# Output projection of two cached attention blocks: weights taken with a column step of four, and the 128x4 results stored directly

## The chip, the cores and the metric

The kernel runs on one core of a Trainium2 chip. The time is the device time of one execution in microseconds; the median of three runs before the change is 671.81 us (671.5 to 672.41). One execution was also recorded by the hardware profiler; its own time is 671.82 us, and its span, from the first to the last instruction, is 670.0 us.

## The reference

Two attention blocks, A and B, of the same shape decode one token each, and their results are put side by side. Cut to what matters:

```
# for each block: x [1,1,512], k_cache and v_cache [1,32,8192,128], wq [512,4096], wo [4096,512], all bf16
q      = (x @ wq) reshaped to 32 heads of 128
scores = q . k_cache / sqrt(128)            # [32, 8192]
p      = softmax(scores)
o      = p @ v_cache                        # [32, 128]
y      = o reshaped to [1, 4096] @ wo       # [1, 512]
out    = concatenate([y_A, y_B])            # [1, 1, 1024] bf16
```

The two caches of the two blocks are 268 MB, so nearly all that is moved is read once and used once.

## The kernel before, in words

The heads are taken in pairs: 16 pairs of block A (n = 0 to 15), then 16 of block B (n = 16 to 31). For one pair the 128 partitions hold 2 heads times 64 runs of 128 cache rows, so that K and V of a pair are tiles of 128 partitions by 16384 bf16, 4 MB each, in two buffers each (`kn`, `vn`). Every load is issued by SP's DMA queue, in the order written in the program: a K load waits until TensorE has reduced the pair two before it, a V load until the products with V of the pair two before it are done.

The work on a pair: VectorE multiplies K by the broadcast query in four pieces (`plan_mul`, L313). TensorE adds up groups of eight columns through an identity matrix (`plan_red`, L322, two halves of 16 matmuls), VectorE finishes the sums (`plan_sr`, L331) and takes the maximum (L337, L343, L346). TensorE spreads the maximum (L356), ScalarE takes exponentials (`plan_exp`, L367). In the next round TensorE sums the denominators (`plan_sum`, L372) and multiplies the probabilities by V (`plan_pv`, L388, 128 small matmuls with V as weights), and VectorE divides (`plan_o`, L398). Engines run their own instruction lists in the written order and meet through semaphores. TensorE's rounds 1 to 30 are a hardware loop; rounds 31 and 32 stand behind it.

At the start the row x is turned into columns by eight matmuls (L277, weights `xrow[0:1, a, c:D:C]`, which is one partition and a column step of C = 4), and the queries are made from wq (L295).

The output projection is at the end of the program. In round 31 (`L1`), ahead of that round's K work, four relayouts bring finished heads into columns (`plan_relayout`: L423 on VectorE, L427 on TensorE, L429 on VectorE), and `plan_wo(0, 0)` runs block A's whole projection: 128 matmuls (L440) of a 128x128 piece of `wo` as weights by one column of `o2`, four output columns for each of 32 heads, accumulated in `qyp` (128 partitions by 4). When it is done, SP issues block B's `wo` into the same buffer `wbuf` in five loads (16, 8, 4, 2 and 2 heads, `load_wo`), and VectorE rounds `qyp` to `yT` after its second multiplication of the round (`plan_y(0)`, L447). Behind round 32 come block B's five groups (`plan_wo(1, g)`, again 128 matmuls in all, each group behind its own load), `plan_y(1)`, and `plan_out`.

Output column n sits in `yT` at partition n mod 128, column n div 128. So `plan_out` transposes: one matmul by the identity into `bmp` (L451, 8 partitions by 128 columns, both blocks at once), one VectorE copy to `out_q` (L454), one DMA on SP of 8 rows of 256 bytes, and SP's wait for it, which ends the program.

Of the kernel before, what the change touches and what calls it, by code (L numbers as in the profile page):

```python
# [8 lines left out]
BF16 = mybir.dt.bfloat16  # L9
F32 = mybir.dt.float32  # L10

P = 128
# [11 lines left out]
class _Plan:  # L24
# [6 lines left out]
    def wait(self, eng, mark):  # L31
        if mark is None:
            return
        ctr, val = mark
        if val <= 0 or self.waited.get((eng, ctr.name), 0) >= val:
            return
        self.waited[(eng, ctr.name)] = val
        self.prog[eng].append((None, ctr, val))

    def op(self, eng, fn, ctr=None, needs=(), inc=1):  # L40

        for m in needs:
            self.wait(eng, m)
        self.prog[eng].append((fn, ctr, inc))
        if ctr is None:
            return None
        ctr.n += inc
        return ctr, ctr.n
# [67 lines left out]
def bass_concat_heads__mha_block_cached__gqa_block_cached__decode_kernel(  # L116
# [18 lines left out]
    NA = 2  # L135
    H, Sk, Dh = ks[0].shape[1:]
    D = xs[0].shape[2]
    NOUT = wos[0].shape[1]
# [8 lines left out]
    NP = NA * PA  # L147
# [10 lines left out]
    with ExitStack() as st:  # L158
# [3 lines left out]
        def sb(name, shape, dt):  # L162
            return ec(nc.sbuf_tensor(name, shape, dt))
# [6 lines left out]
        wo_sb = wbuf[:].rearrange("p (j n) -> p j n", n=NOUT)  # L170
# [7 lines left out]
        ident = sb("ident", [P, P], BF16)  # L178
# [11 lines left out]
        jsel = {g: sb("jsel%d" % g, [P, g], BF16) for g in RG}  # L190
        NQ = NOUT // P
        yT = sb("yT", [P, NA, NQ], BF16)
        out_q = sb("out_q", [NA * NQ, P], BF16)

        def ps(name, shape):
            return ec(nc.psum_tensor(name, shape, F32))
# [4 lines left out]
        bmp = ps("bmp", [P, 512])  # L201
        misc = ps("misc", [P, 512])
        qyp = ps("qyp", [P, 512])

        pl = _Plan()
        op, wait = pl.op, pl.wait

        def ctr(name):
            return _Ctr(nc, st, name)
# [4 lines left out]
        s_v2 = ctr("s_v2")  # L214
        s_k = [ctr("s_k%d" % i) for i in range(NK)]
        s_v = [ctr("s_v%d" % i) for i in range(NV)]
        s_out = ctr("s_out")
        c_pool, c_dve, c_act, c_pe = ctr("c_pool"), ctr("c_dve"), ctr("c_act"), ctr("c_pe")
        c_mul, c_red, c_sr, c_pv = ctr("c_mul"), ctr("c_red"), ctr("c_sr"), ctr("c_pv")

        def dma(eng, dst, src, c, needs=()):
            return op(eng, lambda e: e.dma_start(dst, src), c, needs, inc=16)  # L222


        def const(fn, needs=()):
# [5 lines left out]
            out=ident[:], in_=ones_bf[:], pattern=[[1, P]], compare_op=ALU.is_equal,  # L231
            fill=0.0, base=0, channel_multiplier=-1), [i_onesb])
        i_identf = const(lambda e: e.affine_select(
            out=ident_f[:], in_=ones_f[:], pattern=[[1, P]], compare_op=ALU.is_equal,
# [12 lines left out]
        def load_k(n):  # L247
            a, i = divmod(n, PA)
            src = ks[a][0, 2 * i:2 * i + 2].rearrange("h (p t) d -> (h p) (t d)", p=HP)
            k_in[n] = dma("SP", kn[:, n % NK].rearrange("p t d -> p (t d)"), src, s_k[n % NK],  # L250
                          [red_done.get(n - NK)])
# [14 lines left out]
        def load_wo(a, g):  # L266
            h0, n = WOG[a][g]
            src = wos[a][h0 * Dh:(h0 + n) * Dh, :].rearrange("(p j) n -> p (j n)", p=P)
            wo_in[a, g] = dma("SP", wo_sb[:, h0:h0 + n, :].rearrange("p j n -> p (j n)"), src, s_wo[g],
                              [q_done[0] if a == 0 else wo_done[0]])  # L270


        for a in range(NA):
# [6 lines left out]
            m = op("PE", xmm, c_pe, [x_in, i_onesb])  # L280
            x_ready = op("ACT", lambda e, a=a: e.copy(
                xb[:, a].rearrange("p c m -> p (c m)"), (misc if a == 0 else qyp)[:]), c_act, [m])
        misc_free, qy_free = [x_ready], [x_ready]
# [3 lines left out]
        def plan_q(a, j):  # L287

            def mm(e):
                r = None  # L290
                for hh in range(2):
                    for c in range(C):
                        w = wq_sb[a][:, c, 8 * j * Dh:8 * (j + 1) * Dh].rearrange(
                            "p (i h d) -> p i h d", h=2, d=Dh)[:, :, hh, :]
                        r = e.matmul(  # L295
                            qyp[hh * HP:(hh + 1) * HP, :].rearrange("p (i d) -> p i d", d=Dh),
                            xb[:, a, c, hh * HP:(hh + 1) * HP], w,
                            start=(c == 0), stop=(c == C - 1))
                return r
            m = op("PE", mm, c_pe, [x_ready, wq_in[a], qy_free[0]])  # L300
            q_done[a] = m
            n0 = a * PA + 4 * j
            qy_free[0] = op("ACT", lambda e: e.copy(  # L303
                qbc[:, n0:n0 + 4, :].rearrange("p i d -> p (i d)"), qyp[:]), c_act, [m])
            for n in range(n0, n0 + 4):
                qbc_ready[n] = qy_free[0]
# [43 lines left out]
        nb_done = {}  # L350
# [66 lines left out]
        def plan_relayout(a, g):  # L417
            h0, n = WOG[a][g]
            z = z_n[0] % 2
            z_n[0] += 1  # L420
            s = P // n
            zv = zb[:, z, :].rearrange("p (h s) -> p h s", s=s)
            m = op("DVE", lambda e: e.tensor_tensor(  # L423
                zv, oD[:, a, h0:h0 + n].unsqueeze(2).broadcast_to([P, n, s]),
                mask[n][:, None, :].broadcast_to([P, n, s]), ALU.mult),
                c_dve, [sel_ready[n], o_done[a * PA + (h0 + n) // 2 - 1], z_free.get(z)])
            z_free[z] = op("PE", lambda e: e.matmul(misc[:, 0:n], zb[:, z, :], jsel[n][:],  # L427
                                                    start=True, stop=True), c_pe, [m, misc_free[0]])
            o2_ready[a, g] = misc_free[0] = op("DVE", lambda e: e.tensor_copy(  # L429
                o2[:, a, h0:h0 + n], misc[:, 0:n]), c_dve, [z_free[z]])  # L430

        def plan_wo(a, g):

            h0, n = WOG[a][g]

            def mm(e):
                r = None
                for j in range(h0, h0 + n):
                    for i in range(NQ):
                        r = e.matmul(qyp[:, i:i + 1], wo_sb[:, j, i * P:(i + 1) * P],  # L440
                                     o2[:, a, j:j + 1], start=(j == 0 and i == 0),
                                     stop=(j == H - 1 and i == NQ - 1), skip_group_check=True)
                return r
            wo_done[a] = op("PE", mm, c_pe, [o2_ready[a, g], wo_in[a, g], qy_free[0]])

        def plan_y(a):
            qy_free[0] = op("DVE", lambda e: e.tensor_copy(yT[:, a, :], qyp[:, 0:NQ]), c_dve,  # L447
                            [wo_done[a]])

        def plan_out():  # L450
            m = op("PE", lambda e: e.matmul(bmp[0:NA * NQ, 0:P], yT[:].rearrange("p a q -> p (a q)"),  # L451
                                            ident[:], start=True, stop=True),
                   c_pe, [qy_free[0], nb_done[NP - 1]])
            m = op("DVE", lambda e: e.tensor_copy(out_q[:], bmp[0:NA * NQ, 0:P]), c_dve, [m])  # L454
            done = dma("SP", out[0].rearrange("o (q n) -> (o q) n", q=NA * NQ), out_q[:], s_out, [m])
            wait("SP", done)


        L0, L1 = 1, 31
# [8 lines left out]
        for n in range(NP + 1):  # L468
            marks[n] = len(pl.prog["PE"])
            last = n == NP  # L470
            if n == L1:
                plan_relayout(0, 0)
                for g in range(3):
                    plan_relayout(1, g)
                plan_wo(0, 0)
            if n + 1 < NP:
                load_k(n + 1)
            if n == 1:
                for j in range(4):
                    plan_q(1, j)  # L480
                marks[n] = len(pl.prog["PE"])
            if not last:
                load_v(n, 2 if n == NP - 1 else 1)
            if n == 12:
                load_wo(0, 0)
            if n == NP - 1:
                for g in range(len(WOG[1])):
                    load_wo(1, g)
            if not last:
                plan_mul(n, 0)  # L490
                plan_mul(n, 1)
            if n == L1:
                plan_y(0)
            if n > 0:
                plan_sum(n - 1)
            if not last:
                plan_red(n, 0)
                plan_mul(n, 2)
                plan_mul(n, 3)
                plan_sr(n, 0)  # L500
                plan_red(n, 1)
            if n > 0:
                plan_pv(n - 1, 0, HT)
            if not last:
                plan_sr(n, 1)
                plan_max(n)
                plan_gmax(n)
            if n > 0:
                plan_pv(n - 1, HT, T)
            if not last:  # L510
                plan_exp(n)
            if n > 0:
                plan_o(n - 1)
            if n >= L1:
                plan_relayout(1, n - L1 + 3)
        for g in range(len(WOG[1])):
            plan_wo(1, g)
        plan_y(1)
        plan_out()

        for name, at in (("SP", block.sync), ("PE", block.tensor), ("ACT", block.scalar),
                         ("DVE", block.vector), ("POOL", block.gpsimd)):
# [37 lines left out]
```

## Time and profile before

| | |
|---|---|
| median of three runs | 671.81 us |
| profiled execution, its own time | 671.82 us |
| its span | 670.0 us |
| TensorE (matmuls) busy | 473.1 us, 71% |
| VectorE busy | 359.6 us, 54% |
| ScalarE busy | 43.9 us, 7% |
| moved by DMA | 285.39 MB, mean 426 GB/s |
| projection matmuls (L440) | 256 of 165 ns on average |

The profile cuts the span into 40 slices of 16.75 us and gives the busy share of each engine in tenths. Groups are named by line, engine, operation and by output and inputs. "PEld" is the loading of weights into TensorE, which lies beside the matmuls. "SPq" and "ACTq" are DMAs issued by those engines; the time given for one is that of issuing it. The chain that ended last is followed back from the last instruction to what released each step. Wait lists say for whom an engine stood idle. The granted TensorE clock (PEclk) is given as a share of full speed.

### The profile page before, as it was taken

To read this page: it belongs to the slowest core of one execution; us is meant where nothing else is said; L and a number is where in the kernel's file an instruction comes from. 1 tells how busy PE (TensorE), PEld (TensorE's weight loads), DVE (VectorE), ACT (ScalarE), POOL (GpSimd) and SP (SyncE) were. 2 spreads that over 40 slices of the span, in tenths; PEclk is the share of its full clock that TensorE was granted. 3 is DMA by queue.
4 is the path that set the end of the run, shared out by engine and by line. 5 is a ranking of instruction groups with operands and counts; after the bars stand their busy time and mean duration, and the time that the engine had idled before them with its cause. 6 is when DMAs were issued, how large, how long until landed. Compare 5 with 4: busy or idle time off the path is not lost.

```text
span 670.0 us, 12431 instructions
## 1 busy us (share of the span) xinstructions
PE 473.1 (71%) x5711; PEld 276.2 (41%) x5711; DVE 359.6 (54%) x345; ACT 43.9 (7%) x171; POOL 2.1 (0%) x13
## 2 busy tenths in 40 slices
PE   2677876766777776664667776676687766768887
PEld 1224443434444343441344443344454334444456
DVE  1545456665555666515655556665555656555561
ACT  1120000000000000000000000000000000000000
POOL 1000000000000000000000000000000000000000
PEclk9977876667787666786677876667878766788766
DMA  9999999999999999999999999999999999999996
GB/s 376 438 433 422 427 436 435 432 428 425 439 434 434 426 425 436 438 430 430 423 436 438 430 430 425 436 436 432 430 425 436 436 431 428 428 434 434 433 416 272
DMA packets 10545, 285.39 MB, mean 426 GB/s; under 512 B 1186, under 2 KB 1188, under 8 KB 1572
## 3 DMA queue, kind: packets, MB, share of 16 engines
q1 hardware_dynamic: 10528, 285.22, 99.1%
q8 instruction: 8, 0.13, 0.1%
q14 instruction: 5, 0.04, 0.0%
q10 hardware_dynamic: 4, 0.00, 0.0%
HBM read 285.21 MB, written 0.00 MB: 426 GB/s over the span
## 4 chain that ended last, share of the span: by engine, by line
DMA 65%; PE 23%; DVE 7%; issue 4%; SPq 0%
DMA kn<-in_A_k_cache_dram 31%; DMA kn<-in_B_k_cache_dram 30%; PE rps L322 22%; DVE kn L313 7%; DMA wbuf<-in_B_wo_dram 3%; PE qyp L440 1%; PE acc L388 0%; SPq L222 0%; PE bmp L356 0%; PE misc L427 0%; DVE zb L423 0%; DVE o L429 0%; PE mtp L343 0%; PE bmp L451 0%; DVE out_q L454 0%
## 5 line engine op out<-in xcount | busy, mean ns | idle before, releaser
L322 PE MATMUL rps<-kn,ident 128*128 128x512 bf16 x1024 | 294.6, 459 | 134.6 <-DVE kn L313 134.6
L313 DVE TENSOR_TENSOR kn<-kn,qbc 128x4096 bf16<-128x4096 bf16 x128 | 286.8, 2283 | 88.4 <-DMA kn<-in_A_k_cache_dram 59.0
L322 PEld LDWEIGHTS rps<-kn,ident 128*128 128x128 bf16 x1024 | 114.6, 115 | 302.5 <-DVE kn L313 132.6
L388 PEld LDWEIGHTS acc<-pt,vn 128*128 128x128 bf16 x4096 | 110.5, 97 | 14.3 <-issue 6.9
L331 DVE TENSOR_REDUCE s_sb<-rps 128x64 f32<-128x512 f32 x64 | 44.3, 692 | 132.2 <-PE rps L322 132.2
L388 PE MATMUL acc<-pt,vn 128*128 128x2 bf16 x4096 | 112.8, 163 | 0.0
L372 PE MATMUL misc<-rsum,ones_f 128*128 128x2 f32 x64 | 18.2, 355 | 39.5 <-ACT pt L367 38.8
L360 ACT ACTIVATE negb<-bmp 128x1 f32<-128x1 f32 x32 | 5.5, 171 | 587.8 <-PE bmp L356 587.8
L372 PEld LDWEIGHTS misc<-rsum,ones_f 128*128 128x128 f32 x64 | 15.5, 301 | 42.9 <-ACT pt L367 41.3
L398 DVE TENSOR_TENSOR oD<-acc,rinv 128x2 bf16<-128x2 f32 x32 | 5.1, 160 | 47.6 <-PE acc L388 47.6
L367 ACT ACTIVATE pt<-s_sb,negb 64x128 bf16<-64x128 f32 x64 | 27.8, 435 | 1.9
L346 DVE TENSOR_REDUCE gm<-mtp 1x2 f32<-1x128 f32 x32 | 8.9, 279 | 27.8 <-PE mtp L343 27.8
L356 PE MATMUL bmp<-gm,hrow 1*128 1x1 f32 x128 | 23.2, 282 | 0.5 <-DVE gm L346 0.5
L356 PEld LDWEIGHTS bmp<-gm,hrow 1*128 1x128 f32 x128 | 20.6, 226 | 1.3 <-issue 0.7
L343 PE MATMUL mtp<-ident_f,m 128*1 128x128 f32 x64 | 12.1, 271 | 1.1 <-DVE m L337 1.1
L295 PE MATMUL qyp<-wbuf,xb 128*64 128x512 bf16 x32 | 7.7, 632 | 6.2 <-DMA wbuf<-in_A_wq_dram 4.1
L367 ACT ACTIVATION_READ_ACCUMULATOR pt<-s_sb,negb 64x1 f32 x64 | 11.6, 182 | 0.0
L337 DVE TENSOR_REDUCE m<-s_sb 128x1 f32<-128x128 f32 x32 | 9.2, 286 | 1.1
L295 PE MATMUL qyp<-vn,xb 128*64 128x512 bf16 x32 | 6.6, 554 | 2.3 <-ACT qbc L303 2.3
L440 PE MATMUL qyp<-o,wbuf 128*128 128x1 bf16 x256 | 7.6, 165 | 0.5 <-DMA wbuf<-in_B_wo_dram 0.3
L440 PEld LDWEIGHTS qyp<-o,wbuf 128*128 128x128 bf16 x256 | 7.2, 104 | 0.7 <-issue 0.4
L375 DVE RECIPROCAL rinv<-misc 128x2 f32<-128x2 f32 x32 | 5.3, 164 | 3.4 <-PE misc L372 3.4
(34 smaller groups left out, 27.4 us busy)
## 6 DMA issues: line engine op xcount, KB each, us to landing
kn<-in_A_k_cache_dram SPq DMA_DIRECT2D x16, 4096.0 KB, 25.3
vn<-in_A_v_cache_dram SPq DMA_DIRECT2D x16, 4096.0 KB, 31.4
kn<-in_B_k_cache_dram SPq DMA_DIRECT2D x16, 4096.0 KB, 25.4
vn<-in_B_v_cache_dram SPq DMA_DIRECT2D x15, 4096.0 KB, 31.5
wbuf<-in_A_wq_dram SPq DMA_DIRECT2D x1, 4096.0 KB, 12.4
vn<-in_B_wq_dram SPq DMA_DIRECT2D x1, 4096.0 KB, 30.8
wbuf<-in_A_wo_dram SPq DMA_DIRECT2D x1, 4096.0 KB, 41.2
vn<-in_B_v_cache_dram SPq DMA_DIRECT2D x2, 2048.0 KB, 18.5
```

Of the source, the lines that this page charges most:

```text
L295: r = e.matmul(qyp[hh * HP:(hh + 1) * HP, :].rearrange("p (i d) -> p i d", d=Dh), xb[:, a, c, hh * HP:(hh + 1) * HP], w, start=(c == 0), s ...
L313: mul_done[n, c] = op("DVE", lambda e: e.tensor_tensor(k, k, qbc[:, n:n + 1, :].broadcast_to([P, CT, Dh]), ALU.mult), c_mul, [k_in[n], qbc ...
L322: r = e.matmul(rps[:, h, :].rearrange("p (t d) -> p t d", d=DW), ident[:], kn[:, n % NK, h * HT:(h + 1) * HT, i * DW:(i + 1) * DW], start= ...
L331: sr_done[n, h] = op("DVE", lambda e: e.tensor_reduce(s_sb[:, n % 2, h * HT:(h + 1) * HT], rps[:, h, :].rearrange("p (t d) -> p t d", d=DW ...
L337: m_done[n] = op("DVE", lambda e: e.tensor_reduce(m1[:, n % 2:n % 2 + 1], s_sb[:, n % 2, :], AX.X, ALU.max), c_dve, [sr_done[n, 1]])
L343: m = op("PE", lambda e: e.matmul(mtp[0:1, 0:P], m1[:, n % 2:n % 2 + 1], ident_f[:], start=True, stop=True), c_pe, [m_done[n], i_identf, g ...
L346: gm_done[n] = op("DVE", lambda e: e.tensor_reduce(gm[:, n % 2, :], mtp[0:1, 0:P].rearrange("o (h p) -> o h p", h=2), AX.X, ALU.max), c_dv ...
L356: r = e.matmul(bmp[:, 0:1], hrow[0:1, h, :], gm[0:1, n % 2, h:h + 1], start=(h == 0), stop=(h == 1))
L367: p_done[n] = op("ACT", lambda e, h=h, q=q: e.activation(pt[q, n % 2, :, h], s_sb[q, n % 2, :], AF.Exp, bias=negb[q, n:n + 1], scale=scale ...
L372: m = op("PE", lambda e: e.matmul(misc[:, 0:2], ones_f[:], rsum[:, n % 2, :], start=True, stop=True), c_pe, [p_done[n], misc_free[0]])
L388: r = e.matmul(acc[:, n % 2, 0:2], vn[:, n % NV, t, :], pt[:, n % 2, t, :], start=(t == 0), stop=(t == T - 1))
L440: r = e.matmul(qyp[:, i:i + 1], wo_sb[:, j, i * P:(i + 1) * P], o2[:, a, j:j + 1], start=(j == 0 and i == 0), stop=(j == H - 1 and i == NQ ...
```

## The change

Three things are edited. First, `plan_wo` takes as weights the columns i, i+4, i+8 and so on of `wo` instead of a run of 128, so that partition p of `qyp` holds outputs 4p to 4p+3. Second, `plan_out` with its transposing matmul, its copy and its DMA is gone. Third, `store_y` writes the 128x4 tile `yT` of one block as it is, 8 bytes from each of 128 partitions: block A's on ACT's queue in round 31, behind `plan_y(0)`, block B's on SP's queue behind `plan_y(1)`. SP waits for B's store at the end, ACT for A's.

```
-        out_q = sb("out_q", [NA * NQ, P], BF16)
...
-        s_out = ctr("s_out")
+        s_out = [ctr("s_out%d" % a) for a in range(NA)]
...
-                        r = e.matmul(qyp[:, i:i + 1], wo_sb[:, j, i * P:(i + 1) * P],
+                        r = e.matmul(qyp[:, i:i + 1], wo_sb[:, j, i:NOUT:NQ],
                                      o2[:, a, j:j + 1], start=(j == 0 and i == 0),
                                      stop=(j == H - 1 and i == NQ - 1), skip_group_check=True)
...
-        def plan_out():
-            m = op("PE", lambda e: e.matmul(bmp[0:NA * NQ, 0:P], yT[:].rearrange("p a q -> p (a q)"),
-                                            ident[:], start=True, stop=True),
-                   c_pe, [qy_free[0], nb_done[NP - 1]])
-            m = op("DVE", lambda e: e.tensor_copy(out_q[:], bmp[0:NA * NQ, 0:P]), c_dve, [m])
-            done = dma("SP", out[0].rearrange("o (q n) -> (o q) n", q=NA * NQ), out_q[:], s_out, [m])
-            wait("SP", done)
+        def store_y(a, eng):
+            return dma(eng, out[0, 0, a * NOUT:(a + 1) * NOUT].rearrange("(p q) -> p q", q=NQ),
+                       yT[:, a, :], s_out[a], [qy_free[0]])
...
             if n == L1:
                 plan_y(0)
+                a_out = store_y(0, "ACT")
...
         plan_y(1)
-        plan_out()
+        wait("SP", store_y(1, "SP"))
+        wait("ACT", a_out)
```

## The prediction

> **What bounds the kernel now.** I read the page's slices first, then the last part of the chain that ended last, then the timeline around the two places where `wo` is multiplied, the waits there, and the rows of the weight loads. The slices:
>
> ```profile
> DMA  9999999999999999999999999999999999999996
> GB/s 376 438 433 422 427 436 435 432 428 425 439 434 434 426 425 436 438 430 430 423 436 438 430 430 425 436 436 432 430 425 436 436 431 428 428 434 434 433 416 272
> ```
>
> The DMA engines are full in every slice but the last. The change issues no other load, so only the last 35 us can move: the end of the last load and what lies behind it. The chain over that end (start, duration, what):
>
> ```profile
> 645.18 21.87 DMA wbuf<-in_B_wo_dram
> 667.05 0.14 issue
> 667.19 0.37 PE qyp L440 x8
> 667.56 0.02 issue
> 667.58 0.17 DVE yT L447
> 667.75 0.04 issue
> 667.80 0.28 PE bmp L451
> 668.08 0.02 issue
> 668.11 0.28 DVE out_q L454
> ```
>
> The last piece of B's `wo` lands at 667.05; eight matmuls, the rounding, the transpose and the second copy follow one after another. Next come the store's issue, the wait for its landing, and the rest of the span:
>
> ```profile
> 668.41 0.37 SPq L222 DMA_DIRECT2D out_dram<-out_q  x1
> ```
>
> ```profile
> SPq L158 <- DMA out_dram<-out_q: 0.9, 1, 0.9
> ```
>
> How near TensorE is to the load, and what A's projection stands before, is in the timeline (idle time before a group and its releaser in brackets):
>
> ```profile
> 639.18 4.48 DVE L313 TENSOR_TENSOR kn<-kn,qbc 128x4096 bf16<-128x4096 bf16 x2
> ...
> 643.58 0.15 DVE L447 CAST yT<-qyp 128x4 bf16<-128x4 f32 x1
> ...
> 643.72 9.34 PE L322 MATMUL rps<-kn,ident 128*128 128x512 bf16 x32 [0.82 <-DVE kn L313]
> ...
> 657.22 0.17 ACT L360 ACTIVATE negb<-bmp 128x1 f32<-128x1 f32 x1 [19.03 <-PE bmp L356]
> ...
> 667.19 0.35 PE L440 MATMUL qyp<-o,wbuf 128*128 128x1 bf16 x8 [0.34 <-DMA wbuf<-in_B_wo_dram]
> ```
>
> TensorE has 0.82 us of slack behind A's projection, and 0.34 us before B's last eight matmuls. Those two figures decide what slower weight loads would cost.
>
> **The change, part by part.** The sum is made against the profiled execution, 671.82 us (span 670.0 and 1.8 around it); the runs' median, 671.81, is the same to 0.01.
>
> *Removed from the end.* `yT` is done at 667.75, and the store is issued at 668.41. Between lie 0.04 + 0.28 + 0.02 + 0.28 + 0.02 = 0.64 us of hand-overs, matmul and copy; one hand-over of 0.02 stays. Nothing lies beside them, as no other engine works after 667.56, so all of it goes: -0.64. What is late next is the store itself. B's landing at 667.05 stays ahead of it.
>
> *The last store, its issue.* It took 0.37 us for 8 rows. A's 128-partition loads are issued in 0.41 to 0.53 us at the start and the wo loads in 0.327 at best, 0.432 in the middle (1.3 at most, where the queue was full). An issue depends little on the rows: I take 0.43, that is +0.06, between -0.04 and +0.16.
>
> *The last store, its transfer.* From the issue's end, 668.78, to SP's release at 669.66 are 0.88 us. The transfer's window shows 16 packets, in the packet records eight of 256 bytes at 15 to 16 ns and eight completion words of 4 bytes at 7 to 9 ns, all within 0.1 us around 669.25; so most of the 0.88 is start and receipt (0.36 behind the last packet). Afterwards it is 128 packets of 8 bytes; over 16 engines that is eight on each where it was at most one. By the nearest rows they cost 7 x 9 to 7 x 16 ns, 0.06 to 0.11 us. The trace has no store of 8 bytes. Lower end -0.05 (the same packets closer together); upper end, if each of an engine's writes waited for the receipt of the one before, 7 x 0.36 = +2.5. The packet records are the same kind of write through the same queue, differing only in size, and a 4-byte write is among them, so I take +0.10 and keep the 2.5 as a rival.
>
> *The first store.* It is issued on ACT at 643.75, behind `plan_y(0)`. ACT has no work until 657.22 (it waits 19.03 us there), so the issue, 0.21 to 0.52 us in the rows of the x loads on the same queue, and the wait for `yT` delay nobody. Its 128 packets share the DMA engines, which are full there: 8 x 9 to 8 x 16 ns plus a completion word is 0.08 to 0.14 us of each engine, and those engines set the landing at 667.05. The lower end is 0, if the slowest engine is not delayed by it; the upper is 8 x 0.36 = +2.9, if an engine stood still for each receipt. I take +0.10 by the packet rows. The five `wo` issues on SP fall at 642.51 to 645.18, beside it; should they come half a microsecond later, the V load issued at 636 still feeds the engines until 655. ACT's wait at the end meets a store long landed.
>
> *The strided weights.* 256 loads of 128 columns now step over four elements, 8 bytes. The trace of before has such loads: `xrow` is taken with a step of four in L277, in one partition. Those and the contiguous loads of the same size (minimum, median, maximum in ns):
>
> ```profile
> L277 PEld LDWEIGHTS misc<-ones_bf,xrow x4: 108/134/142, 8.1 to 8.3; 1*128 1x128 bf16 x4
> ```
>
> ```profile
> L440 PEld LDWEIGHTS qyp<-o,wbuf x256: 103/104/118, 638.9 to 667.4; 128*128 128x128 bf16 x128
> ```
>
> ```profile
> L343 PEld LDWEIGHTS mtp<-ident_f,m x64: 79/81/83, 37.1 to 654.6; 128*1 128x1 f32 x64
> ```
>
> A load of one column takes 81 ns, one of 128 contiguous columns 104: reading columns is seen in this duration. The first strided load, which found TensorE idle, took 108; the later ones (134 to 142) stand behind matmuls of 128 columns and tell nothing. So a step of four adds some 4 ns. L440's pairs of load and matmul follow each other every 26.6 ns (128 in 3.40 us). A gain is excluded, because the same count of instructions is issued; the lower end is 0. The upper end is the row of 128 columns of f32 (L372, median 288), +184 ns a pair, but nothing in the diff changes the element size, so the strided row is far nearer. At +4 ns, A's 128 pairs take 0.51 us more, inside the 0.82 (VectorE's copy has 1.1 us as well): 0. B's first 120 take 0.48 more, of which 0.34 is covered by the last landing, and the last eight 0.03: +0.17.
>
> *Sum*: -0.64 + 0.06 + 0.10 + 0.10 + 0.17 = -0.21 us, that is 671.6. One `yT` copy, the semaphores and the ACT wait change nothing else that the chain contains.
>
> [...]
>
> **The rivals.**
>
> 1. *Small writes cost a round trip each.* Place: the last store, between 667.77 and SP's release. For it: 8-byte neighbours from different engines meet in the same stretch of memory, and no row shows that. Against it: the 4-byte completion words take 9 ns. Price: full, -0.21 - 0.10 + 2.5 = +2.2, 674.0; half of it 672.8. It decides (over +1.34 us) when the transfer takes 1.65 us more than before. The first store alone could do the same through the landing, as its engines are full.
>
> 2. *The strided load is read at a lower rate with 128 partitions* (ends on the slower side). For it: L277 is one partition, four loads, never at the 26.6 ns pace. Against it: 108 against 104 ns. Price at twice the pace, 26.6 ns more a pair: A's projection ends 3.4 later, less 0.82 = +2.6, which TensorE carries through its unbroken row of `rps` and `acc` matmuls to B's projection; there +3.2 - 0.34 + 0.2; with the other terms -0.38 the sum is +5.3, 677.1. Past 6.4 ns a pair both slacks are gone and the cost is 256x - 1.16 us; it decides from x = 11 ns. At +184 ns it would be some 717.
>
> 3. *All costs at their lower ends*: -0.64 - 0.04 - 0.05 = -0.73, 671.1; still no difference that can be told. For more than -1.34 even the landing at 667.05 would have to move, which nothing in the change brings about.
>
> **How the numbers follow.** A measurement of this kernel tells about 0.2%, 1.34 us, from no change. Chances: the forecast with rival 3, all between 671.1 and 672.5, 70%; rival 1, 15% (a third of it within 0.2%); rival 2, 11%; something faster than the removed steps, 4%. That gives faster 0.04, same 0.70 + 0.05 = 0.75, slower 0.10 + 0.11 = 0.21. The range goes from 670.9, the lower ends less the spread of 0.3 of the runs below their median, to 674.0, rival 1 in full; rival 2, the 4% and the few points of rival 1 in which the first store is slow too are left out.
>
> **What would show it.** Right: L440's loads at 104 to 110 ns and the row of eight at 0.37; A's projection done in under 4.2 us; nothing between `yT` and SP's issue; an issue near 0.4 and an SP wait near 1.0; a landing of `wbuf` within 0.2 of 667.05. Wrong: a wait of SP beyond 2.5 us (rival 1); L440 pairs more than 37 ns apart, the idle 0.82 and 0.34 gone and the chain running through TensorE from 639 on (rival 2); a landing several tenths later after the store at 643.8.

## The result, and the profile after

The changed kernel takes 674.53 us (median of 6 runs, 674.15 to 675.19) against 671.71 us for the kernel before in the same comparison (671.5 to 672.41): a ratio of 1.0040 with a 95% interval of 1.0027 to 1.0053, 2.8 us slower. The forecast of 671.6 and the range up to 674.0 are both missed. The profiled execution took 674.15 us, with a span of 672.4 us, 2.4 more than before.

The chain of the kernel after, over its end (start, duration, what):

```profile
643.75 24.28 DMA wbuf<-in_B_wo_dram
668.03 0.14 issue
668.17 0.41 PE qyp L439 x8
668.58 0.02 issue
668.60 0.16 DVE yT L446
```

The transpose and the copy are gone as they should be. But the last piece of `wo` lands at 668.03 where it landed at 667.05, although its issue is over 1.4 us earlier. What follows the chain is the store and the wait for it, from SP's timeline and SP's list of waits:

```profile
668.79 0.35 SPq L221 DMA_DIRECT2D out_dram<-yT  x1
```

```profile
SPq L158 <- DMA out_dram<-yT: 2.9, 1, 2.9
```

The store is issued 0.38 us later than before (668.79 against 668.41), and SP waits 2.9 us for it instead of 0.9 (in the packet records SP goes on 2.2 us after the last packet of the store, where it was 0.38). Together 0.38 + 2.0 = 2.4 us, the whole difference of the two profiled spans (the medians differ by 2.8). Of the 0.38, +0.98 is the landing, +0.04 the eight slower matmuls, and -0.64 the removed steps.

Why the load lands later can be seen in the stretches behind A's early store, issued at 642.34. Of the kernel before, then of the kernel after (stretch, its length, busy time and count by engine, granted clock, DMA share, GB/s):

```profile
648.00:650.00 2.00, 2.00 (x10) 0.90 (x9) 0.56 (x2) 0.00 (x0) 0.00 (x0) 0.92 1.03 434
650.00:652.00 2.00, 2.00 (x11) 0.88 (x9) 0.34 (x1) 0.00 (x0) 0.00 (x0) 1.00 0.98 410
```

```profile
648.00:650.00 2.00, 2.00 (x11) 0.94 (x10) 0.69 (x1) 0.00 (x0) 0.00 (x0) 1.00 1.43 262
650.00:652.00 2.00, 2.00 (x30) 1.18 (x29) 0.35 (x1) 0.00 (x0) 0.00 (x0) 1.00 0.52 205
```

The engines count as busy as ever (1.43 and 0.52 average to 0.98: a packet counts where it begins), but move little more than half as much. In the packet records the 16 KB packets of the V load that begin at 648 to 650 us take 1417 ns on average, where they take 622 before. The 8-byte packets themselves are entered with 9 ns. They do not come at once, but are spread over 645.9 to 652.5 us, between the packets of the loads; up to 648 us, with 59 of the 128 written, the loads still move 426 GB/s. At 656 us 4.30 MB stand in load packets that are not complete, against 3.66 before; at 425 GB/s those 0.64 MB are 1.5 us. The landing moved by less, 0.98. That the rest fitted into a tail in which the engines are not full (87 GB/s before and 238 after, from 664 to 667 us) is likely, but no run shows it.

The weight loads:

```profile
L439 PEld LDWEIGHTS qyp<-o,wbuf x256: 110/118/132, 637.5 to 668.4; 128*128 128x128 bf16 x128
```

They take 118 ns in the median, not 104. A's 128 pairs take 4.28 us in the chain, 33.4 ns a pair, where they took 3.43. TensorE does not set the end, though: it waits for the loads of B's `wo` at three places:

```profile
PE qyp L439 <- DMA wbuf<-in_B_wo_dram: 1.8, 3, 1.2
```

### The profile page after: what moved, and what is told of

Same layout as the page of the kernel before. It is cut to its first block, busy times and chain, and to the rows that moved or that the text cites. A ratio compares the mean times of both kernels' runs of the same rounds, so it can differ in the third digit from the quotient of the medians.

```text
span 672.4 us, 12430 instructions
## 1 busy us (share of the span) xinstructions
PE 474.3 (71%) x5710; PEld 277.8 (41%) x5710; DVE 359.3 (53%) x344; ACT 43.9 (7%) x171; POOL 2.1 (0%) x13
## 4 chain that ended last, share of the span: by engine, by line
DMA 60%; PE 27%; DVE 7%; issue 4%; ACT 0%; SPq 0%
DMA kn<-in_B_k_cache_dram 30%; DMA kn<-in_A_k_cache_dram 27%; PE rps L321 24%; DVE kn L312 7%; DMA wbuf<-in_B_wo_dram 4%; PE qyp L294 1%; PE acc L387 1%; PE qyp L439 1%; ACT qbc L302 0%; SPq L221 0%; PE bmp L355 0%; PE mtp L342 0%; PE misc L426 0%; DVE s_sb L330 0%; DVE zb L422 0%
## 5 line engine op out<-in xcount | busy, mean ns | idle before, releaser
L439 PE MATMUL qyp<-o,wbuf 128*128 128x1 bf16 x256 | 9.3, 172 | 1.8 <-DMA wbuf<-in_B_wo_dram 1.8
L439 PEld LDWEIGHTS qyp<-o,wbuf 128*128 128x128 bf16 x256 | 9.0, 118 | 2.0 <-DMA wbuf<-in_B_wo_dram 1.6
```

The lines of the kernel that those rows point to most:

```text
L439: r = e.matmul(qyp[:, i:i + 1], wo_sb[:, j, i:NOUT:NQ], o2[:, a, j:j + 1], start=(j == 0 and i == 0), stop=(j == H - 1 and i == NQ - 1), s ...
```

## The experiments

Receipt is used here for the time from the last packet of a store to the release of the engine that waits for it. Theory S: the 8-byte stores cost twice, by a late receipt at the end and by stalling the loads among which the first is written. Rivals: W, the slower strided loads push the end; V, the later landing is the spread of one execution. Later, among the stores, the count of small pieces (C) against small pieces whose neighbours are written at the same time (H). Differences are to the kernel before on the same chip: 671.66 us for the first four runs of the table and for the last, 671.64 for the two others.

| run | median us | ratio to before, 95% interval |
|---|---|---|
| strided weights alone | 671.64 | 0.9996, 0.9987 to 1.0005 |
| both 8-byte stores alone | 674.74 | 1.0044, 1.0030 to 1.0058 |
| early store alone, added | 674.01 | 1.0033, 1.0020 to 1.0045 |
| change, A's store moved to the end | 674.03 | 1.0032, 1.0020 to 1.0044 |
| change, A's store left out | 673.13 | 1.0024, 1.0014 to 1.0034 |
| change with 16-byte pieces | 671.73 | 1.0005, 0.9994 to 1.0016 |
| A's half stored early in 256-byte rows | 671.75 | 0.9999, 0.9991 to 1.0008 |

### The strided weights alone

```
-  r = e.matmul(qyp[:, i:i + 1], wo_sb[:, j, i * P:(i + 1) * P],
+  r = e.matmul(qyp[:, i:i + 1], wo_sb[:, j, i:NOUT:NQ],
```

> The kernel before with the strided weights alone; transpose, copy and the 8x256-byte store as before, so the outputs come out in another order (the reordering is left out). Theory S: the pairs run at 34 ns; A's projection takes 4.4 us instead of 3.4, of which 0.82 was slack, B's 120 pairs ahead of the last landing take 0.9 more against 0.34 of slack: +0.1 to +0.9 us, and SP waits 0.9 us at the end. Theory W: +2 us or more.

The weight loads run as in the changed kernel, and the time does not move. The row of this run:

```profile
L440 PEld LDWEIGHTS qyp<-o,wbuf x256: 111/118/133, 637.5 to 667.2; 128*128 128x128 bf16 x128
```

The chain of this run still goes through the last landing:

```profile
643.87 23.00 DMA wbuf<-in_B_wo_dram
666.87 0.14 issue
667.01 0.41 PE qyp L440 x8
```

W falls: 33 ns a pair cost nothing here, less even than the +0.1 to +0.9 that S expected, because the last landing (666.87 in this run) still comes after TensorE is ready.

### Both stores alone

```
-  wo_sb[:, j, i:NOUT:NQ]          # the changed kernel
+  wo_sb[:, j, i * P:(i + 1) * P]
```

> The changed kernel with the contiguous weights of before; both 8-byte stores as in the change (the outputs come out in another order). Theory S: SP's end wait 2.9 us, load packets slowed at 646 to 652 us, landing about 1 us later than before; -0.64 + 2.0 + 1.0 to 1.8 gives +2.3 to +3.2 us, as much as the whole change. Theory W: -0.6 to +0.5 us.

+3.1 us, as much as the whole change, as S says. The last landing, and SP's wait:

```profile
645.21 23.29 DMA wbuf<-in_B_wo_dram
```

```profile
SPq L158 <- DMA out_dram<-yT: 2.6, 1, 2.6
```

The last piece lands at 668.50, and SP waits 2.6 us. With the contiguous weights the kernel is no faster than the changed one, and the strided weights alone cost nothing: the whole loss lies in the stores.

### The early store alone

The kernel before, with A's `yT` also stored in 8-byte pieces on ACT's queue in round 31:

```
   plan_y(0)
+  a_out = store_y(0, "ACT")
...
   def plan_out():
+      wait("SP", a_out)
```

> The kernel before with one thing added: A's yT is also stored as 128 pieces of 8 bytes on ACT's queue in round 31, and the first half of the output is written again by the ordinary store at the end (so A's half is stored twice). Theory S: load packets at 646 to 652 us take about twice their 615 ns, some 1.8 us of transfer is lost there, and the time rises by 0.8 to 1.9 us with the landing, with SP's end wait unchanged at 0.9. Theory V: no change, -0.4 to +0.4.

+2.35 us, a little over the upper end expected. The chain of this run, then the stretches of it:

```profile
643.75 25.29 DMA wbuf<-in_B_wo_dram
669.04 0.14 issue
```

```profile
648.00:650.00 2.00, 2.00 (x11) 0.89 (x10) 0.69 (x1) 0.00 (x0) 0.00 (x0) 1.00 1.25 312
650.00:652.00 2.00, 2.00 (x34) 1.22 (x32) 0.43 (x1) 0.00 (x0) 0.00 (x0) 1.00 0.75 246
652.00:654.00 2.00, 2.00 (x73) 1.76 (x70) 0.82 (x3) 0.00 (x0) 0.00 (x0) 1.00 1.02 287
```

In this run one kilobyte of 8-byte writes took the loads to between 246 and 312 GB/s for some six microseconds, and the last landing went from 667.05 to 669.04. V falls: the six runs lie between 673.80 and 674.14, all above the slowest of the 17 of the kernel before (673.11). SP's wait at the end stays at 0.9 us, because the last store there is the old one.

### The late store alone, and both stores late

In the first kernel A's store is left out, in the second it is issued on SP just ahead of B's:

```
-  a_out = store_y(0, "ACT")
...
-  wait("ACT", a_out)
```

> The changed kernel without A's early store (A's half of the output is left unwritten); B's 8-byte store at the end stays. Theory H: load packets undisturbed, landing at 666.9 to 667.1, SP's end wait 2.2 to 3.0: -0.64 + 1.4 to 2.1 and the strided loads at 0 to 0.2, that is +0.7 to +1.7 us. If the early store costs nothing by itself: +2.8.

```
-  a_out = store_y(0, "ACT")
...
-  wait("SP", store_y(1, "SP"))
-  wait("ACT", a_out)
+  y_out = [store_y(a, "SP") for a in range(NA)]
+  for m in y_out:
+      wait("SP", m)
```

> The changed kernel, but A's 128x4 store is issued on SP behind B's rounding, just ahead of B's store; nothing is written while loads run. Theory S (8-byte writes are slow in two places: a late receipt of some 2.0 us at the end, and a stall of the load engines when they are written among loads): the stall is gone, the last wo piece lands at 667.0 to 667.3 as before, the packets of 646 to 652 us stay at 615 ns, SP still waits 2.5 to 4 us at the end; with -0.64 for the removed transpose that is +1.4 to +2.8 us on the kernel before, and some 1 us less than the changed kernel if the end wait stays at 2.9. Theory W (the slower strided weight loads, 34 ns a pair against 26.6, push the end): the landing and the time stay as in the changed kernel, +2.8. Theory V (the later landing of 668.03 is the ordinary spread of one execution): the landing stays between 667 and 668 whatever is moved.

The late store alone costs +1.5 us, on the chip where the kernel before took 671.64; with the removed 0.64 that is 2.1 for the store, worked out from the time. Its SP wait:

```profile
SPq L158 <- DMA out_dram<-yT: 2.8, 1, 2.8
```

In this execution 120 of the 128 packets end by 668.63, but the other eight begin at 669.70, right behind a 16 KB load of instructions (668.45 to 669.69). SP goes on 2.2 us after the 120 and 1.0 us after the eight, so this profile alone does not tell which of them held it. In the changed kernel all 128 lie together, with 2.2 us behind them.

The loads are undisturbed in both kernels (422 and 410 GB/s at 648 to 652 us). Two late stores cost +2.4. The issue of the pair takes 0.82 us where one took 0.35, which is about half of what the second store adds; the rest is not taken apart. The gain on the changed kernel is about half a microsecond, not the whole one that S expected, and is not clear of the noise (1.0032 against 1.0040, with intervals that overlap). The profile of that second kernel also shows what the slower weights do when TensorE is late: B's 128 pairs run unbroken and end the chain.

```profile
664.24 4.27 PE qyp L439 x128
```

That execution, 674.71, is the slowest of its six. The early store alone (+2.35) and the late store alone (+1.5) add up to 3.85 us, more than both together cost (+3.1, or +2.8 in the changed kernel); no run shows why.

### 16 bytes a piece

`yT` is made eight columns wide, and each store writes 128 pieces of 16 bytes over the whole output, at the same places and on the same queues. As both now write the same bytes, SP waits for A's store before it issues B's:

```
-  yT = sb("yT", [P, NA, NQ], BF16)
+  yT = sb("yT", [P, NA, 2 * NQ], BF16)
...
-  out[0, 0, a * NOUT:(a + 1) * NOUT].rearrange("(p q) -> p q", q=NQ)
+  out[0, 0, :].rearrange("(p q) -> p q", q=2 * NQ)
...
-  wait("SP", store_y(1, "SP"))
-  wait("ACT", a_out)
+  wait("SP", a_out)
+  wait("SP", store_y(1, "SP"))
```

> The changed kernel with pieces of 16 bytes instead of 8: yT holds eight columns a block (the other four are old numbers), and each store writes 128 pieces of 16 bytes over the whole output, at the same two places and on the same queues; the result is not the right one. As many pieces, twice the bytes. Theory H (a piece of 8 bytes whose neighbours are written at the same time is slow, one of 16 is not): no stalled load packets at 646 to 652 us, landing near 667.0, SP's end wait 1.0 to 1.1 us, so -0.64 + 0.1 to 0.3 = -0.6 to -0.2 us on the kernel before. Theory C (the count of small pieces is what costs): as the changed kernel, +2.5 to +3.2.

With as many pieces and twice the bytes, the stall is gone and SP's wait is 1.1 us, 0.2 above that of the kernel before. SP's wait, then the stretches:

```profile
SPq L158 <- DMA out_dram<-yT: 1.1, 1, 1.1
```

```profile
648.00:650.00 2.00, 2.00 (x9) 0.85 (x8) 0.53 (x2) 0.00 (x0) 0.00 (x0) 0.80 0.99 402
650.00:652.00 2.00, 2.00 (x11) 0.92 (x10) 0.61 (x1) 0.00 (x0) 0.00 (x0) 1.00 1.01 426
```

So C falls: 128 pieces of 16 bytes left the loads at 402 and 426 GB/s and the wait at 1.1 us. But the gain expected (-0.6 to -0.2) did not come; the median is 0.1 above before. The chain of the profiled execution shows one reason: the projection with its strided loads runs unbroken (33.4 ns a pair) into the rounding, so here the slower weights do cost time.

```profile
663.98 3.61 PE qyp L439 x108
667.59 0.02 issue
667.62 0.17 DVE yT L446
```

`yT` is done at 667.79, no earlier than before. The runs spread from 671.16 to 673.84 and the interval reaches 0.4 us below no change, so how much of the 0.64 is left is not settled.

### Early, in rows of 256 bytes

In short, on the kernel before:

```
   plan_y(0)
+  a_out = store_t()     # matmul by the identity, copy, store of 4 rows of 256 bytes on ACT
```

> The kernel before, with A's half also transposed in round 31 (one more matmul and copy) and stored there on ACT's queue as 4 pieces of 256 bytes; the end is as before. If it is the 8-byte pieces that stall the load engines, nothing is stalled here: packets stay at 615 ns at 646 to 652 us, and the time rises by 0 to 0.6 us (TensorE and VectorE hand over once more in round 31). If any write among loads stalls them, +0.8 to +1.9 us.

No difference, and no stall:

```profile
648.00:650.00 2.00, 2.00 (x11) 0.91 (x10) 0.69 (x1) 0.00 (x0) 0.00 (x0) 1.00 0.98 410
650.00:652.00 2.00, 2.00 (x36) 1.29 (x35) 0.53 (x1) 0.00 (x0) 0.00 (x0) 1.00 0.92 393
```

Four rows of 256 bytes written among the loads cost no time that shows (0.9999), with the loads at 410 and 393 GB/s. It is also no gain, since the end still waits for B alone.

### Sizes and distances

Two kernels put further stores behind the old last one, one at a time on SP, each waiting for the one before. The first kernel, in short:

```
+  for n, w, step in LADDER:      # pieces, elements in a piece, elements from piece to piece
+      dst = out[0, 0, 0:n * (step or w)].rearrange("(p q) -> p q", q=step or w)[:, 0:w]
+      m = dma("SP", dst, lad[0:n, 0:w], s_out, [m])
```

> The kernel before, with fourteen more stores to the output behind its own last one, one after another on SP, each waiting for the landing of the one before; they hold other numbers and overwrite the result. Widths and counts: 8 pieces of 256 bytes; 128 of 8 next to each other; 128 of 8 at a step of 16 bytes; 64, 32 and 16 of 8; 16 of 8 at a step of 128 bytes; 1 of 8; 128 of 16; 64 of 16; 64 of 32; 32 of 64; 16 of 128; 8 of 256 again. From an issue to the landing: 8 of 256 bytes about 1.3 us (0.37 + 0.9), 128 of 8 about 3.2. Theory P (each write below some size costs its engine a round trip, one after another): the time grows with the pieces an engine gets, 1 of 8 and 16 of 8 (one each) stay near 1.3 to 1.6, 64 and 32 of 8 lie between, and a step of 16 or 128 bytes changes nothing. Theory N (writes of neighbours into the same stretch of memory wait for each other): 128 of 8 at a step of 16 is shorter than side by side, 16 of 8 at a step of 128 is shorter than 16 side by side, which are slow. Theory G (any piece of 8 bytes has a long receipt): 1 of 8 takes about 3 us too.

> The kernel before with twenty-one further stores one after another behind its own, in another order than in the first series, with some repeated: 1 of 8 bytes; 16 of 8 at a step of 128; 128 of 16; 128 of 8; 8 of 256; 16 of 8 side by side, at steps of 16, 32 and 64 bytes; 32 of 8 side by side, at 32 and at 64; 64 of 8 side by side and at 32; 128 of 8 at 16; 64 of 16 side by side and at 32; 128 of 8, 16 of 8 at 128, 128 of 16 and 8 of 256 again. Theory H: those of 8 bytes side by side wait 1.4 to 3.4 us from their last packet to the release in whatever order, those of 16 bytes 0.4 to 0.5, and the first step at which pieces of 8 wait only 0.4 us tells the length of the stretch that neighbours share (16, 32, 64 or 128 bytes). If the first series was slow by its order (a store behind many others), the times do not follow the shapes here.

From SP's timeline, the store of 128 times 8 bytes and the next one in the first kernel:

```profile
670.84 0.36 SPq L223 DMA_DIRECT2D out_dram<-lad  x1
...
673.56 0.36 SPq L223 DMA_DIRECT2D out_dram<-lad  x1
```

It takes 2.72 us from issue to issue. The wait behind the last packet in the records, in microseconds, by shape; where there are several numbers the shape was measured more than once:

| pieces | side by side | step 16 B | step 32 B | step 64 B | step 128 B |
|---|---|---|---|---|---|
| 1 of 8 B | 0.32, 0.32 | | | | |
| 16 of 8 B | 1.47, 0.37 | 1.18 | 0.74 | 0.37 | 0.38, 0.37, 0.38 |
| 32 of 8 B | 3.40, 2.24 | | 0.38 | 0.38 | |
| 64 of 8 B | 2.81, 2.36 | | 0.40 | | |
| 128 of 8 B | 1.67, 2.42, 2.01 | 1.10, 0.80 | | | |
| 64 of 16 B | 0.53, 0.43 | | 0.40 | | |
| 128 of 16 B | 0.42, 0.42, 0.42 | | | | |
| 64 of 32 B, 32 of 64 B, 16 of 128 B | 0.40, 0.38, 0.39 | | | | |
| 8 of 256 B, four stores with the kernels' own | 0.37 to 0.38 | | | | |

Two 256-byte stores that stood last in their kernels are not in the table; there too SP goes on after 0.37 and 0.38 us. Pieces of 8 bytes waited 1.47 to 3.40 us side by side (with one exception, 16 pieces at 0.37) and 0.80 to 1.18 at a step of 16 bytes; at a step of 64 or 128 they waited 0.37 to 0.38, no longer than the rows of 256 bytes, one piece alone 0.32, and pieces of 16 bytes side by side 0.42 to 0.53. It is not a matter of order, as the second kernel repeats the shapes in another order. A round trip for each of an engine's pieces, one after another, does not fit either: 32 pieces side by side, two on an engine if 16 engines share them evenly, waited 2.24 and 3.40, and 128, eight on an engine, 1.67 to 2.42. Two things stay open: at which step the longer wait ends (at a step of 32 bytes 16 pieces waited 0.74, 32 and 64 pieces 0.38 and 0.40), and why 16 pieces side by side took 1.47 us once and 0.37 once. Each shape was measured one to three times, and the waits of one shape differ by up to 1.2 us. What makes pieces side by side wait longer no run shows.

### The step of the weight loads

A's 128 loads were taken in four blocks of 32, with steps of 1, 2, 4 and 8 elements, each on a line of its own (shown in short; step 1 is L443, which also holds B's 128 loads):

```
+  wbuf[:, k * 256:k * 256 + 256:2]       # L446; L449: step 4, L452: step 8
```

> The kernel before, with A's 128 weight loads of the projection taken at four column steps, 32 loads each: 1, 2, 4 and 8 elements (A's outputs hold other numbers; B's loads and both transposes stay). If the time of a load follows the lines of memory that it touches, the loads take 104 ns at a step of 1, 118 at 4 as in the changed kernel, less at 2 and clearly more at 8 (130 to 200 ns), and pairs follow every 26.6, 27 to 31, 34 and 40 to 70 ns. If a step of any size costs the same, 2, 4 and 8 all lie at 118 and 34.

The groups of this run (line, engine, operation, tiles, shape and count; busy time, mean ns of one):

```profile
L443 PEld LDWEIGHTS qyp<-o,wbuf 128*128 128x128 bf16 x160 | 4.6, 104 | 0.4 <-issue 0.4
L452 PEld LDWEIGHTS qyp<-o,wbuf 128*128 128x128 bf16 x32 | 2.0, 167 | 0.0
L449 PEld LDWEIGHTS qyp<-o,wbuf 128*128 128x128 bf16 x32 | 1.1, 116 | 0.0
L446 PEld LDWEIGHTS qyp<-o,wbuf 128*128 128x128 bf16 x32 | 0.9, 104 | 0.0
```

A step of 2 took the 104 ns of a step of 1, 4 took 12 ns a load more and 8 took 63 more, all in one execution. From 2 to 8 the time grew with the step, as the first of the two expectations had it; that the lines of memory are the reason is not shown.

## Why the prediction was wrong

*Removed from the end, -0.64.* Right: rounding done at 668.76, store issued at 668.79.

*Issue of the last store, +0.06.* Right in kind, with the other sign: 0.35 instead of 0.37, inside the bounds.

*Transfer of the last store, +0.10.* The step that failed first. It argued that "the packet records are the same kind of write through the same queue, differing only in size, and a 4-byte write is among them". The packets are indeed 9 ns, and all 128 lie within 0.2 us; the cost is not in a packet's duration but behind the last one, where no row of before could show it. The 4-byte completion words that were the argument, 7 to 9 ns, told as little of that wait, and a single 8-byte piece is quick too (0.32). Measured: SP's wait +2.0 (2.2 us behind the last packet instead of 0.38), and 2.1 by the time of the run with the late store alone. The upper end of +2.5 was near in size, but for another reason than the one it was worked out from.

*The first store, +0.10.* The second failure, for the same reason, the price taken from the duration of a packet: +1.0 in the landing of the profiled execution, +2.35 when it is the only change. The upper bound, 2.9 us, did hold, though no engine stood still once for each piece: with 59 of the 128 pieces written, the loads still ran at 426 GB/s. Why it is more alone (landing 669.04) than with the rest (668.50 and 668.03) is not settled; the load left over at 656 us differs in the same sense, 4.53, 4.43 and 4.30 MB.

*The strided weights, +4 ns a pair.* Mis-sized: +14 ns on the load, 6.6 ns on the pair. The single strided row, four loads of one partition at a slack moment, did not show the pace; in the changed kernel too the four loads that found TensorE idle took 110 to 114 ns, and the median of all is 118. The term's effect, +0.17, was not far off: the strided weights alone measured 0 (0.9987 to 1.0005), because the landing covers them. Where the landing does not, as in the profiled executions of the two late stores and of the 16-byte pieces, B's 128 pairs end the chain and cost time. Rival 2 decided from 11 ns, and that was not reached.

*The rivals.* Rival 1 happened, in both places at once. It was priced at the last store alone (+2.2), with one sentence that the first store "could do the same". The case that both are slow was seen, called a "few points" and left out of the range, and no price was put on it; the range therefore ended at 674.0, with the 674.5 outside. One cause that acts in two places is one case and should have been priced as a sum: -0.64 + 2.5 + 2.9 = +4.8 as the upper end. It was half right: that each piece waits for the receipt of the one before does not fit the store series (32 pieces side by side 2.24 and 3.40 us, 128 pieces 1.67 to 2.42), but how close the pieces lie, which its "for it" sentence named, did make the difference (32 pieces at a step of 32 bytes 0.38); by what mechanism no run shows.

## What to carry to other kernels

Before a store is made simpler, look at how long its pieces are and what lies next to them: 128 pieces of 8 bytes side by side cost 2 us of receipt at the end of this program, and 1.0 to 2.4 us when written among full loads, against 0.64 us for the transpose that made rows of 256 bytes. Here a packet's own duration (9 ns) did not show what the writes cost; the wait behind their store did (2.2 us against 0.38), and so did the rate of the other transfers meanwhile (205 GB/s against 410). And when one unknown cost enters at two places, price both together.

## What the runs showed of the hardware

Not expected: in the changed kernel a kilobyte of 8-byte writes brought full loads down to 205 GB/s over two microseconds, where they moved 410 before, while the DMA share, averaged with the stretch before, showed no loss (0.98). In the store series pieces of 8 bytes at a step of 64 bytes had a receipt of 0.37 and 0.38 us and pieces of 16 bytes side by side one of 0.42 to 0.53, where pieces of 8 bytes side by side had 1.47 to 3.40 (and 0.37 once).

The weight loads of 128 columns at steps of 1, 2, 4 and 8 bf16 elements took 104, 104, 116 and 167 ns. Four was the first of these steps at which a load took longer, by 12 ns.
